# Moving a product behind the masks and scaling values earlier, at the border of two tiles of a fused attention and SwiGLU kernel

## The chip, the cores and the metric

The kernel runs on one core of a Trainium2 chip. The metric is the device time of one execution in microseconds (us). Before the change it is 238.01 us, the median of three runs (237.95 to 238.2).

## What is computed

The reference has two stages. The first is linear attention with a decay for each head, over q, k and v of shape (4, 8, 768, 64) (batch, heads, positions, head size) and a vector lam of 8 decays, in blocks of 64 positions:

```
for b in range(nb):
    intra = einsum('bhic,bhjc->bhij', qb, kb) * Dmask
    intra = einsum('bhij,bhjd->bhid', intra, vb)
    inter = einsum('bhid,bhde->bhie', qb * lam_pow, kv_state)
    out[:, :, sl] = intra + inter
    kb_dec = kb * rev_pow
    kv_state = lam_block * kv_state + einsum('bhsd,bhse->bhde', kb_dec, vb)
```

The second takes the attention's output as 3072 tokens of 512 numbers and applies a feed-forward stage of width 1536: `(silu(x @ w_gate) * (x @ w_val)) @ w_out`. The result is 3072 x 512 in float32. The kernel may choose its own block length, since a longer block gives the same sums.

## The kernel before

**Tiles.** The 768 positions are cut into six tiles of 128 positions. A tile holds all four batches, which the code calls blocks b = 0 to 3, so it has 512 tokens. Heads are kept in pairs: `kbd` and `vbd` hold k and v of a pair in a block-diagonal form, in three slots that the tiles use in turn. The first two tiles (tt = 0 and 1) are computed as one block of 128 positions, the later four as two halves of 64.

**Attention of a tile**, block by block:
- `prep_k` and `prep_q` turn k and q with TensorE (PE) in the first three tiles, or two for q; later tiles are turned by transposing transfers, issued on SP's queue by `turn` (L230, L234). `scale` multiplies the turned q by powers of the decay on VectorE (DVE), giving `qt` (L222, L224).
- `front` multiplies k and q on PE into `sp` in PSUM (L256, L258; from the third tile on L247) and masks it on DVE into `ssb` (L260; L249). The PSUM pool of `sp` has two buffers; for a block of the first two tiles `front` uses both.
- `values` adds what the state gives (`kvb`, L277; L272) and what the masked scores give (`vbd`, L278, L280; L273) into `op`, and ScalarE (ACT) copies it to `xt`, the input of the feed-forward stage (L287). For the last block of a tile of the first two, the copy is split: ACT copies two of four head pairs (L284) and DVE the other two (L285). DVE's half waits for ACT's.
- The state: `scale_v` multiplies v by powers of the decay into `v_s` (L300), two instructions to a block, on DVE for the first two tiles and on GpSimd (POOL) for the later ones. `update` multiplies k and `v_s` on PE into `up` (L313), DVE adds it to the decayed state `kvd` (L317) and decays it again (L321), and `cast_kv` copies it to `kvb` on ACT (L325). From the third tile on, `update_mid` (L333, L336) and `update_end` (midd L353, kv L355, kvd L357) do this for the two halves.

**Feed-forward of a tile.** `ffn_fc` is called twelve times, for 128 of the 1536 columns each: four gate matmuls into `gp` (L369), SiLU on ACT into `sil` (L371), four value matmuls into `vp` (L374), and the product of the two on DVE into `h_sb` (L375). `gp` and `vp` take turns in a PSUM pool of three buffers. `ffn_out` is called for each block: twelve matmuls into `ffn_op` (L384), a copy on ACT into `osb` (L387) and a transfer out on SP's queue (L388).

**The order is written out by hand.** The pools of tiles are managed, and waits are derived from them, but each engine runs its instructions in the order in which the program issues them. For each tile the loop makes a list of units: the twelve `ffn_fc`, and from the second tile on, after every third, one `ffn_out` of the tile before. So the second tile's units are 0, 1, 2: `ffn_fc`; 3: `ffn_out`; 4, 5, 6: `ffn_fc`; 7: `ffn_out`, and so on to 15. Behind each unit it issues the pieces of attention that a table names for that unit. The table `first` holds those of the first tile's units, `second` those of the second's. Pieces in them work ahead: at the end of `first` stand `front` and `values` of the second tile (L449), and from unit 4 of `second` on, the third tile's attention begins (`turn`, then `spread`).

In `second`, before the change, each block's `scale_v` is issued one or two units ahead of its `update`:

```
for b, (s0, s1) in enumerate(((0, 1), (1, 3), (3, 4), (4, 5))):
    add(second, s0, scale_v, 1, b)
    add(second, s1, update, 1, b)
    add(second, s1 + 1, cast_kv, b)
```

In the first tile's last unit, `ffn_fc` issues its `h_sb` product at once, in front of `front` for blocks 2 and 3 of the second tile, which are pieces of that unit (`first[11]`).

POOL's queue issues all loads, each waiting for the transfer eight before it, and the products of `scale_v` from the third tile on. Its order is: v of the second tile, `w_out`, k, q and v of the third tile, `scale_v` of the third tile's blocks 0 and 1, k and q of the fourth tile, `scale_v` of the third tile's blocks 2 and 3, v of the fourth, and so on.

Of the kernel before, what the change touches and what calls it, by code (L numbers as in the profile page):

```python
# [21 lines left out]
def kernel(  # L22
# [24 lines left out]
    FC = DFF // 128  # L47
# [48 lines left out]
    def load_tile(tt, order, b0=0, b1=B):  # L96
        for t in order:
            if t is q:
                if b0 == 0:
                    qn[tt] = load.tile([128, B, H, D], BF16, name="q_nat", tag="q_nat")  # L100
                load_q(tt, b0, b1)
            else:
                for c in range(2):
                    load_bd(t, kbd if t is k else vbd, tt, c, b0, b1)
# [93 lines left out]
    def xt_of(tt):  # L198
        if tt not in xts:
            xts[tt] = xpool.tile([128, MC, TT], BF16, name="xt", tag="xt")  # L200
        return xts[tt]
# [89 lines left out]
    def scale_v(tt, b):  # L291

        v_s = att.tile([128, HP, 2, D], BF16, name="v_s", tag="v_h" if tt >= HALF else "v_s")
        for h, ps in enumerate(HALVES):
            vb = vbd[ps, tt % SLOTS, 0, b * HP, 64 * h:64 * h + 64]
            eng = nc.gpsimd if tt >= HALF else nc.vector
            n = 1 if tt == NBLK - 1 else 2
            pv = bap(pw[ps], [[7, HP], [0, n], [0, D]], extra_offset=3) if tt >= HALF else \
                bap(pw[ps], [[7, HP], [1, n], [0, D]], extra_offset=2)
            eng.tensor_tensor(out=v_s[ps, :, 0:n], in0=bap(vb, [[128, HP], [128 * NP, n], [1, D]]), in1=pv,  # L300
                              op=ALU.mult)
        scaled[tt, b] = v_s
# [54 lines left out]
        nc.vector.tensor_tensor(out=kvd[b], in0=kvn[b], in1=lam64, op=ALU.mult)  # L357


    hs = {}  # L360

    def ffn_fc(tt, fc):
        xt = xt_of(tt)
        if fc == 0:
            hs[tt] = hpool.tile([128, FC, TT], BF16, name="h_sb", tag="h")
        fs = slice(fc * 128, (fc + 1) * 128)
        gp = gpsum.tile([128, TT], FP32, name="gp", tag="g")
        for mc in range(MC):
            nc.tensor.matmul(gp, wg_sb[:, mc, fs], xt[:, mc, :], start=(mc == 0), stop=(mc == MC - 1))  # L369
        sil = opool.tile([128, TT], BF16, name="sil", tag="sil")  # L370
        nc.scalar.activation(sil, gp, AF.Silu)  # L371
        vp = gpsum.tile([128, TT], FP32, name="vp", tag="g")
        for mc in range(MC):
            nc.tensor.matmul(vp, wv_sb[:, mc, fs], xt[:, mc, :], start=(mc == 0), stop=(mc == MC - 1))  # L374
        nc.vector.tensor_tensor(out=hs[tt][:, fc, :], in0=sil, in1=vp, op=ALU.mult)  # L375

    def ffn_out(tt, b, i=0, parts=1):

        w = DM // parts
        cs = slice(i * w, (i + 1) * w)  # L380
        t0 = b * S + tt * BLK
        op = apsum.tile([128, w], FP32, name="ffn_op", tag="a")
        for fc in range(FC):
            nc.tensor.matmul(op, hs[tt][:, fc, b * BLK:(b + 1) * BLK], wo_sb[:, fc, cs],  # L384
                             start=(fc == 0), stop=(fc == FC - 1))
        osb = opool.tile([128, w], FP32, name="osb", tag="osb")
        nc.scalar.copy(out=osb, in_=op)  # L387
        nc.sync.dma_start(out=out[t0:t0 + BLK, cs], in_=osb)  # L388
# [32 lines left out]
    def add(at, i, *piece):  # L421
        at.setdefault(i, []).append(piece)

    def spread(tt, at, slots):

        for b, (s0, s1, s2, s3, s4) in enumerate(slots):
            if tt >= TURNED:
                add(at, s0, scale_q, tt, b)
            else:
                add(at, s0, prep_k, tt, b)  # L430
                add(at, s1, scale_q, tt, b)
            add(at, s1, update_mid, tt, b)
            add(at, s2, cast_mid, b)
            add(at, s2, front, tt, b)
            add(at, s2, update_end, tt, b)
            add(at, s3, values, tt, b)
            if tt + 1 < NBLK:
                add(at, s4, cast_kv, b)

    first = {}  # L440
# [5 lines left out]
    for i, f, b in ((7, prep_k, 0), (8, prep_k, 1), (8, prep_q, 0), (9, prep_k, 2), (9, prep_q, 1), (9, front, 0),  # L446
                    (10, front, 1), (10, prep_q, 2), (10, prep_k, 3), (10, prep_q, 3)):
        add(first, i, f, 1, b)
    first[11] = [(front, 1, 2), (values, 1, 0), (front, 1, 3), (values, 1, 1), (values, 1, 2), (values, 1, 3, True)]  # L449
    second = {}  # L450
    for b, (s0, s1) in enumerate(((0, 1), (1, 3), (3, 4), (4, 5))):
        add(second, s0, scale_v, 1, b)
        add(second, s1, update, 1, b)
        add(second, s1 + 1, cast_kv, b)

# [2 lines left out]

    for tt in range(NBLK):
        units = [(ffn_fc, tt, fc) for fc in range(FC)]  # L460
        if tt:
            units = sum([units[3 * b:3 * b + 3] + [(ffn_out, tt - 1, b)] for b in range(B)], [])
        pieces = {}
        if tt < 2:
            pieces = (first, second)[tt]
        elif tt + 1 < NBLK:
            spread(tt + 1, pieces, [(i - 1, i, i + 1, i + 2, i + 3)
                                    for i in ((2, 5, 9, 12) if tt == 2 else (1, 4, 8, 12))])
        if 0 < tt < NBLK - 1:
            for b in range(2):  # L470
                scale_v(tt + 1, b)
            if tt + 2 < NBLK:
                load_tile(tt + 2, (k, q) if tt == 1 else (v, k, q))
            for b in range(2, B):
                scale_v(tt + 1, b)
            if tt == 1:
                load_tile(3, (v,))
        if tt and TURNED <= tt + 2 < NBLK:
            for part, i in enumerate((9, 10, 12) if tt == 1 else (5, 6, 8)):
                add(pieces, i, turn, tt + 2, part)  # L480
        for i, (f, *at) in enumerate(units):
            f(*at)
            for g, *on in pieces.get(i, []):
                g(*on)
# [34 lines left out]
```

## Time and profile before

| what | value |
|---|---|
| median of three runs | 238.01 us (237.95 to 238.2) |
| the profiled execution: its own time | 238.19 us |
| its span, from the first to the last instruction | 236.4 us |
| granted TensorE clock | 1.0 of full speed |
| PE, busy share of the span | 93% |
| DVE, ACT, POOL, busy share | 52%, 52%, 44% |
| chain that ended last, share of PE | 72% |

The profile is of one execution. Its page gives the busy time of each engine and the chain of work that ended last. Questions to its trace give instructions in order of time (start in us, duration in us, engine, line of the code, operation, output and inputs, and in brackets the idle time before it and what ended it), and waits in total (who waited for whom, us, times, longest). PE's times are modelled: a matmul's shown end lies later than the moment at which the next can start, so that matmuls overlap in the list. Rows of the same kind that follow each other are merged into one, with x and their number.

### The profile page before, as it was taken

How to read it: one execution, taken by the hardware profiler on the slowest of the kernel's cores; microseconds unless marked ns; L12 is line 12 of the kernel's file. 1: busy time of each engine (PE TensorE's matmuls, PEld its weight loads, DVE VectorE, ACT ScalarE, POOL GpSimd, SP SyncE). 2: the span in 40 equal slices, each digit the busy share in tenths (PEclk: the TensorE clock that was granted, in tenths of full speed). 3: DMA queues.
4: the chain of work that ended last, by engine and by line, in shares of the span. 5: the costliest groups of instructions: out<-in, count | busy, mean ns of one | idle time of the engine just before them, and what ended most of it. 6: DMA issues, size and time to landing. Idle time of an engine off the chain costs nothing.

```text
span 236.4 us, 4384 instructions
## 1 busy us (share of the span) xinstructions
PE 220.3 (93%) x1708; PEld 116.3 (49%) x1708; DVE 122.1 (52%) x234; ACT 123.1 (52%) x233; POOL 104.1 (44%) x129
## 2 busy tenths in 40 slices
PE   0498999989899999999999999999999999999994
PEld 0384446734455554554554555554555544444443
DVE  6685796757827954566466447336334412322200
ACT  7775669535576964645644644553634532243112
POOL 7999979962399539999942202200000000000000
PEclk9999999999999999999999999999999999999999
DMA  6999999999959998999999655110110110111032
GB/s 105 192 158 193 206 162 144 142 185 155 188 74 142 175 204 114 169 159 193 146 171 112 133 110 115 47 40 5 47 44 0 47 44 0 44 47 44 16 120 90
DMA packets 105189, 26.51 MB, mean 112 GB/s; under 512 B 96336, under 2 KB 102224, under 8 KB 105168
## 3 DMA queue, kind: packets, MB, share of 16 engines
q0 software_dynamic: 76464, 13.64, 76.1%
q1 hardware_dynamic: 28560, 12.59, 23.4%
q8 instruction: 13, 0.21, 0.4%
q14 instruction: 8, 0.07, 0.1%
q10 hardware_dynamic: 144, 0.00, 0.0%
HBM read 28.32 MB, written 6.29 MB: 146 GB/s over the span
## 4 chain that ended last, share of the span: by engine, by line
PE 72%; DMA 13%; POOL 7%; DVE 3%; issue 1%; ACT 1%; POOLq 0%; ACTq 0%; DVEq 0%
PE ffn_op L384 26%; PE vp L374 20%; PE gp L369 20%; DMA wv_sb<-in_moe_w_val_dram 6%; DMA wo_sb<-in_moe_w_out_dram 5%; DMA vbd<-in_v_dram 2%; POOL vbd L86 2%; POOL kbd L86 2%; DVE v_s L300 2%; PE sp L247 1%; PE op L272 1%; PE op L273 1%; POOL wg_sb L192 1%; PE up L333 1%; POOL wv_sb L192 1%
## 5 line engine op out<-in xcount | busy, mean ns | idle before, releaser
L375 DVE TENSOR_TENSOR h_sb<-sil,vp 128x512 bf16<-128x512 bf16 x72 | 49.3, 687 | 86.0 <-PE vp L374 60.5
L369 PE MATMUL gp<-xt,wg_sb 128*128 128x512 bf16 x288 | 74.0, 379 | 1.0 <-ACT xt L284 0.9
L374 PE MATMUL vp<-xt,wv_sb 128*128 128x512 bf16 x288 | 73.9, 379 | 0.0
L371 ACT ACTIVATE sil<-gp 128x512 bf16<-128x512 f32 x72 | 43.0, 597 | 44.2 <-PE gp L369 42.5
L384 PE MATMUL ffn_op<-wo_sb,h_sb 128*128 128x512 bf16 (+1 forms) x300 | 65.5, 371 | 0.0
L300 POOL TENSOR_TENSOR v_s<-vbd,pw 64x512 bf16<-64x512 bf16 (+1 forms) x32 | 30.4, 950 | 42.2 <-PE up L333 26.0
L374 PEld LDWEIGHTS <-wv_sb 128*128 128x128 bf16 x288 | 28.2, 98 | 34.0
L384 PEld LDWEIGHTS <-h_sb 128*128 128x128 bf16 x300 | 28.3, 98 | 29.5
L387 ACT COPY osb<-ffn_op 128x512 f32<-128x512 f32 (+1 forms) x25 | 14.2, 568 | 52.1 <-PE ffn_op L384 52.1
L369 PEld LDWEIGHTS <-wg_sb 128*128 128x128 bf16 x288 | 25.5, 98 | 25.2 <-issue 1.1
L86 POOL DMA_DIRECT2D vbd<-in_v_dram x32 | 24.2, 795 | 2.0 <-DMA wo_sb<-in_moe_w_out_dram 1.8
L86 POOL DMA_DIRECT2D kbd<-in_k_dram x28 | 22.1, 821 | 2.5 <-DMA wv_sb<-in_moe_w_val_dram 1.7
L287 ACT CAST xt<-op 128x512 bf16<-128x512 f32 x22 | 12.9, 586 | 8.8 <-PE op L273 5.1
L325 ACT CAST kvb<-kv 64x256 bf16<-64x256 f32 x40 | 16.1, 403 | 0.8
L209 ACT CAST ktb<-tk 64x512 bf16<-64x512 f32 x24 | 13.9, 579 | 2.5 <-PE tk L207 2.2
L341 ACT CAST kvb<-mid 64x256 bf16<-64x256 f32 x32 | 12.9, 403 | 0.5
L249 DVE TENSOR_TENSOR ssb<-sp,mask 128x512 bf16<-128x512 f32 x16 | 11.0, 684 | 2.8 <-PE sp L247 2.8
L300 DVE TENSOR_TENSOR v_s<-vbd,pw 64x512 bf16<-64x512 bf16 x16 | 10.9, 683 | 0.2
L214 PE MATMUL tq<-identity,q_nat 128*128 128x128 bf16 x32 | 4.0, 262 | 6.8 <-POOL identity masks.py:199 6.3
L272 PE MATMUL op<-qt,kvb 128*128 128x64 bf16 x128 | 9.8, 193 | 0.1
L273 PE MATMUL op<-ssb,vbd 128*128 128x64 bf16 x128 | 9.8, 193 | 0.0
L272 PEld LDWEIGHTS <-kvb 128*128 128x128 bf16 x128 | 8.7, 98 | 2.1 <-ACT kvb L341 0.2
(78 smaller groups left out, 185.8 us busy)
## 6 DMA issues: line engine op xcount, KB each, us to landing
out_dram<-osb SPq DMA_DIRECT2D x23, 256.0 KB, 2.1
kbd<-in_k_dram POOLq DMA_DIRECT2D x20, 128.0 KB, 6.0
q_nat<-in_q_dram POOLq DMA_DIRECT2D x4, 512.0 KB, 11.0
vbd<-in_v_dram POOLq DMA_DIRECT2D x16, 128.0 KB, 8.2
wo_sb<-in_moe_w_out_dram POOLq DMA_DIRECT2D x1, 1536.0 KB, 13.1
q_raw<-in_q_dram SPq DMA_DIRECT2D x4, 256.0 KB, 5.4
vbd<-in_v_dram POOLq DMA_DIRECT2D x16, 64.0 KB, 4.5
wg_sb<-in_moe_w_gate_dram POOLq DMA_DIRECT2D x2, 512.0 KB, 10.5
```

Source lines behind the costliest of these rows:

```text
L86: nc.gpsimd.dma_start(out=dst[ps, tt % SLOTS, c, b0 * HP:b1 * HP, 64 * h:64 * h + 64], in_=bass.AP(tensor=t.tensor, offset=t.offset + ((b0 ...
L209: nc.scalar.copy(out=ktb[ps, tt % 2, :, b * HP:(b + 1) * HP, 64 * h:64 * h + 64], in_=tk[ps])
L272: nc.tensor.matmul(op[:, hp, cs], kvb[:, c, b, hp, :], qt[:, hp, cs], start=True, stop=False)
L287: nc.scalar.copy(out=xt, in_=op)
L300: eng.tensor_tensor(out=v_s[ps, :, 0:n], in0=bap(vb, [[128, HP], [128 * NP, n], [1, D]]), in1=pv, op=ALU.mult)
L325: nc.scalar.copy(out=kvb[ps, 0, b, :, 64 * h:64 * h + 64], in_=kvn[b][ps])
L369: nc.tensor.matmul(gp, wg_sb[:, mc, fs], xt[:, mc, :], start=(mc == 0), stop=(mc == MC - 1))
L371: nc.scalar.activation(sil, gp, AF.Silu)
L374: nc.tensor.matmul(vp, wv_sb[:, mc, fs], xt[:, mc, :], start=(mc == 0), stop=(mc == MC - 1))
L375: nc.vector.tensor_tensor(out=hs[tt][:, fc, :], in0=sil, in1=vp, op=ALU.mult)
L384: nc.tensor.matmul(op, hs[tt][:, fc, b * BLK:(b + 1) * BLK], wo_sb[:, fc, cs], start=(fc == 0), stop=(fc == FC - 1))
L387: nc.scalar.copy(out=osb, in_=op)
```

## The change

`ffn_fc` is split into `ffn_gv` (gate, SiLU, value) and `ffn_h` (the product into `h_sb`); calling it does both, as before. For the first tile's last unit only `ffn_gv` is called, and its `ffn_h` is issued in `first[11]`, behind `front` of blocks 2 and 3 and `values` of blocks 0 to 2, in front of `values` of block 3. `scale_v` of the second tile's blocks 0 and 1 is issued at the end of `first[11]`, that is ahead of the second tile's units; that of block 2 behind unit 0 and that of block 3 behind unit 2. The updates move one unit forward: from behind units 1, 3, 4, 5 to behind units 0, 2, 3, 4, and their casts with them.

On PE, the four groups of `up` matmuls stand one unit earlier than before and all else keeps its order. On DVE, `h_sb` of the first tile's last unit stands behind four masks; four scalings stand in front of the second tile's first `h_sb`, and the other four behind the first and the second update's instructions. On ACT, the casts stand a unit earlier. The orders on POOL and SP are the same as before. No instruction is added or left out.

```diff
-    hs = {}
-
-    def ffn_fc(tt, fc):
+    hs, gv = {}, {}
+
+    def ffn_gv(tt, fc):
         xt = xt_of(tt)
         if fc == 0:
             hs[tt] = hpool.tile([128, FC, TT], BF16, name="h_sb", tag="h")
...
             nc.tensor.matmul(vp, wv_sb[:, mc, fs], xt[:, mc, :], start=(mc == 0), stop=(mc == MC - 1))
+        gv[tt, fc] = sil, vp
+
+    def ffn_h(tt, fc):
+        sil, vp = gv.pop((tt, fc))
         nc.vector.tensor_tensor(out=hs[tt][:, fc, :], in0=sil, in1=vp, op=ALU.mult)
+
+    def ffn_fc(tt, fc):
+        ffn_gv(tt, fc)
+        ffn_h(tt, fc)
...
-    first[11] = [(front, 1, 2), (values, 1, 0), (front, 1, 3), (values, 1, 1), (values, 1, 2), (values, 1, 3, True)]
+    first[11] = [(front, 1, 2), (values, 1, 0), (front, 1, 3), (values, 1, 1), (values, 1, 2), (ffn_h, 0, FC - 1),
+                 (values, 1, 3, True), (scale_v, 1, 0), (scale_v, 1, 1)]
     second = {}
-    for b, (s0, s1) in enumerate(((0, 1), (1, 3), (3, 4), (4, 5))):
-        add(second, s0, scale_v, 1, b)
+    for b, (s0, s1) in enumerate(((None, 0), (None, 2), (0, 3), (2, 4))):
+        if s0 is not None:
+            add(second, s0, scale_v, 1, b)
         add(second, s1, update, 1, b)
         add(second, s1 + 1, cast_kv, b)
...
         units = [(ffn_fc, tt, fc) for fc in range(FC)]
-        if tt:
+        if tt == 0:
+            units[-1] = (ffn_gv, 0, FC - 1)
+        else:
             units = sum([units[3 * b:3 * b + 3] + [(ffn_out, tt - 1, b)] for b in range(B)], [])
```

## The prediction, as put on record before the run

> **What bounds the kernel now.** I read the page's busy times first, then the waits of PE in the stretch that the change touches, then the order of time of PE, DVE and POOL there.
>
> ```profile
> PE 220.3 (93%) x1708; PEld 116.3 (49%) x1708; DVE 122.1 (52%) x234; ACT 123.1 (52%) x233; POOL 104.1 (44%) x129
> ...
> PE up L313 <- DVE v_s L300: 1.7, 3, 0.7
> PE gp L369 <- ACT xt L284: 0.5, 1, 0.5
> PE sp L256 <- DVE ssb L260: 0.4, 1, 0.4
> PE sp L247 <- DVE qt L224: 0.3, 1, 0.3
> ```
>
> TensorE is busy for 93% of the span, so only a shorter PE wait saves time. The four lower lines are all that PE's matmuls wait for between 43 and 83 us (who is waited for, us in total, times, longest). Before 43 and after 83 us the change leaves every engine's order as it is. The first and third of them are what the change touches.
>
> In order of time, PE's five waits at the border of the first two tiles (start, duration, what ran, idle time in brackets):
>
> ```profile
> 45.15 0.22 PE L256 MATMUL sp<-qt,ktb 128*128 128x128 bf16 x1 [0.41 <-DVE ssb L260]
> 48.09 1.05 PE L369 MATMUL gp<-xt,wg_sb 128*128 128x512 bf16 x4 [0.46 <-ACT xt L284]
> 52.17 0.41 PE L313 MATMUL up<-v_s,kbd 128*128 128x64 bf16 x8 [0.44 <-DVE v_s L300]
> 59.42 0.41 PE L313 MATMUL up<-v_s,kbd 128*128 128x64 bf16 x8 [0.56 <-DVE v_s L300]
> 62.23 0.39 PE L313 MATMUL up<-v_s,kbd 128*128 128x64 bf16 x8 [0.68 <-DVE v_s L300]
> ```
>
> The brackets count from the modelled end of a matmul. Undisturbed, a gate or value pass of four matmuls gives way to the next 0.86 us after its start (the steps of the chain of waits), though its last matmul ends at 1.03. So a wait costs about 0.17 more than its bracket: the three of `up` cost 0.61 (52.17 less 50.70 and 0.86), 0.73 and 0.85 us.
>
> DVE over the same time:
>
> ```profile
> 43.94 0.69 DVE L375 TENSOR_TENSOR h_sb<-sil,vp 128x512 bf16<-128x512 bf16 x1 [0.46 <-PE vp L374]
> 44.54 2.00 DVE L260 TENSOR_TENSOR ssb<-sp,mask 128x384 bf16<-128x384 f32 x4
> 48.07 0.42 DVE L285 CAST xt<-op 128x256 bf16<-128x256 f32 x1 [1.53 <-ACT xt L284]
> 50.11 0.69 DVE L375 TENSOR_TENSOR h_sb<-sil,vp 128x512 bf16<-128x512 bf16 x1 [1.61 <-PE vp L374]
> 50.72 1.40 DVE L300 TENSOR_TENSOR v_s<-vbd,pw 64x512 bf16<-64x512 bf16 x2
> 60.78 1.40 DVE L300 TENSOR_TENSOR v_s<-vbd,pw 64x512 bf16<-64x512 bf16 x2
> ```
>
> Each scaling pair ends 0.05 to 0.06 us before the `up` that waited for it. DVE does not lack time: it idles 1.53 and 1.61 us just before the first pair.
>
> **The change, step by step.** No instruction is added or removed; the orders of SP's and POOL's queues are the same. What changes is places.
>
> (1) The first tile's last h_sb goes behind the masks of blocks 2 and 3. Block 2's first mask then starts when its scores end, 43.81 + 0.19 + 0.04 = 44.04, instead of 44.54. The scores of block 3 wait for that mask to free their PSUM buffer, so they come at 44.65 (PE's preceding values end at 44.57). The values, ACT's copies of xt and the first gate pass follow in the same lockstep: 48.09 becomes 47.59. Saved: 0.50. The h_sb itself now runs at about 46.1 to 46.8, in the 1.53 us in which DVE waits for ACT; its readers (the first output matmuls) come after 53 us, and the PSUM buffer it holds is next wanted at 49.6. Without that idle time it would cost its 0.61 on the xt copy.
>
> (2) Four scaling instructions (blocks 0 and 1) now follow that xt copy at once. DVE: copy 47.57, scalings 47.91 to 50.75 (two pairs by 1.42). The v they read had landed: PE itself read all blocks of it from 44.01 to 47.44. The first `up` follows the gate and value passes at 49.34 instead of waiting to 52.17: its pair is done at 49.31, release 0.05, so 0.02 of 0.61 is left. Saved: 0.59.
>
> (3) Blocks 2 and 3 are scaled well ahead. By adding the rows in the new order, block 2's pair is done at 53.6 and its `up` is due behind the first output matmuls at 56.05; block 3's is done at 57.0, its `up` due at 58.0. Saved: 0.73 + 0.85.
>
> (4) A new wait: the first h_sb of the second tile stands behind the four scalings, so it starts at 50.75 instead of 49.65, and ends 51.44. The third gate pass takes the PSUM buffer that it frees; PE is there at 51.33 and goes on at 51.49. Cost: 0.16. Its bounds: 0 (there is no such wait now) to 1.08, if the scalings ran at 0.91 us each, the longest row of another 512-element bf16 product, qt; all 16 rows of L300 on DVE lie between 676 and 690 ns, so I take 0.16.
>
> Sum at the sixth gate pass: 0.50 + 0.59 + 0.73 + 0.85 - 0.16 = 2.51 us; 62.46 becomes 59.95.
>
> (5) What is late next. Things set by transfers don't move. The third tile's k has landed by 57.5 (issued 47, 9.5 to landing) and is wanted at 61.7; its turned q lands at 67.3 and is wanted at 67.6; v_s of its block 2 leaves POOL at 74.5 and PE wants it at 74.4, which costs 0.1 inside a wait of 0.26 for kvb that is there anyway. The fourth tile's turned q lands at 90.0 when DVE comes for it, some 3 us before PE needs it. These cost nothing.
>
> (6) But DVE now meets POOL elsewhere:
>
> ```profile
> 72.21 4.61 POOL L300 TENSOR_TENSOR v_s<-vbd,pw 64x512 bf16<-64x512 bf16 x4
> ...
> 72.67 0.86 DVE L353 TENSOR_TENSOR midd<-mid,pw 128x256 f32<-128x256 f32 x1
> 74.03 0.70 DVE L357 TENSOR_TENSOR kvd<-kv,pw 128x256 f32<-128x256 f32 x1
> 75.25 0.67 DVE L224 TENSOR_TENSOR qt<-qt,qsc 128x512 bf16<-128x512 bf16 x1
> 77.69 0.41 DVE L353 TENSOR_TENSOR midd<-mid,pw 128x256 f32<-128x256 f32 x1
> 78.60 0.43 DVE L357 TENSOR_TENSOR kvd<-kv,pw 128x256 f32<-128x256 f32 x1
> ```
>
> The same instruction takes 0.41 us alone and 0.86 while POOL multiplies. In POOL's three long stretches of products (72.2 to 76.8, 99.4 to 108.3, 116.6 to 121.1) all eight DVE instructions with both inputs in SBUF are longer, by 0.25 to 0.77 us; those that read PSUM are not. POOL's stretch is set by transfers and stays. The midd, kvd and qt of block 1/2 that ran clear at 77.69 to 79.36 come 2.5 us sooner, at 75.2 to 76.9: midd and at least part of kvd inside it. I take 0.3 to 0.45 for midd and 0 to 0.28 for kvd, together 0.3 to 0.73. The chain has 0.15 us of slack (an h_sb waiting for ACT at 79.76), and then ends in the one place where PE already waits for DVE:
>
> ```profile
> 82.21 0.42 DVE L224 TENSOR_TENSOR qt<-qt,qsc 128x512 bf16<-128x512 bf16 x1
> 82.68 0.39 PE L247 MATMUL sp<-qt,ktb 128*128 128x64 bf16 x8 [0.28 <-DVE qt L224]
> ```
>
> So 0.15 to 0.58 of the gain is given back there; I take 0.46, nearer the upper end because midd's three contended rows (0.86, 0.73, 1.18) are all long. The instructions that leave POOL's stretch (72.67, 74.03) gain PE nothing: it is in output matmuls then.
>
> The Trainium skill, "SBUF — State Buffer", section "Who interferes with whom", has a rule that speaks against the change here: a DVE instruction with two SBUF inputs contends with a GpSimd instruction that reads SBUF, and the loser is blocked for the other's whole instruction. The eight rows agree on who contends, but lengthen by less than a whole POOL product (1.04 to 1.13 us). By that rule my estimate is that midd and kvd would lose about 1.2 us together and the time would be some 236.5; by the rows it is 236.0.
>
> **Sum.** 2.51 - 0.46 = 2.05 us off. The profiled execution took 238.19 us (span 236.4 and 1.8 around it), so 236.14; it lies 0.18 above the median of the runs, 238.01, from which 2.05 leaves 235.96. Predicted: 236.0 us.
>
> **Rivals.**
> Full gain: POOL and DVE don't meet, or the lost time is hidden. For it: kvd and qt are at the edge of POOL's stretch. Against it: eight of eight rows. 238.01 - 2.51 = 235.5.
> Head of the queue: the four scalings hold back the first h_sb for longer, as POOL issues transfers at 48 to 51.4 us. At 0.91 each, 0.92 more: a gain of 1.1, 236.9. Against it: the pair at 50.72 ran beside such issues at its usual 0.68.
> It does nothing: PE's gaps close but the third tile's transfers or POOL's v_s catch PE and take it all back: 238.0. Against it: the dates in (5); only the 0.1 us is missed.
> Slower: the same h_sb behind the four scalings. The savings without it are 2.67 us, so it decides once PE waits longer for that buffer, that is from 0.71 + 0.63 = 1.34 us per scaling on. No row of L300 is so long, POOL's own included (1.135 at most). At 1.5 each, 238.6.
>
> **Chances.** Forecast 0.60 (own range 235.7 to 236.3); full gain 0.17; head of the queue 0.13; nothing 0.05; slower 0.05. A measurement of this kernel can tell 0.2%, 0.48 us, from no change; the head case lies mostly beyond that (0.11 of 0.13). So faster 0.88, same 0.07, slower 0.05. The range, 235.4 to 236.9, reaches from the full gain to the price of the head case.
>
> **What would show it.** (1): the first gate pass of the second tile near 47.6. (2), (3): no PE wait for v_s at L313 above 0.1. (4): a wait of about 0.16 of L369 for h_sb. (6): midd near 75.2 at 0.7 us or more, and PE's wait for qt at L247 grown from 0.28. What would make it wrong: scalings on DVE longer than 0.69, or a PE wait for a transfer or for POOL in the third tile.

## The result, and the profile after

The changed kernel takes 236.47 us, the median of 22 runs (235.49 to 242.68), against 238.14 us for the kernel before on the same chip (22 runs, 237.7 to 239.71). The ratio is 0.9928 [0.9909, 0.9947]: some 1.7 us off, where 2.05 was predicted. The ratio leaves out the three longest runs of the changed kernel (239.22 to 242.68 us), of which the longest had a lower granted clock (0.993). Two more series of the changed kernel, below, gave 0.9929 and 0.9924. The time lies inside the predicted range. What is to be explained is a gain about a third of a microsecond short (the 2.05 itself lies inside each interval), and runs that spread more than before: the median lies 0.98 us above the lowest run after the change and 0.44 before it, and from lowest to lowest the gain is 2.21 us (237.70 to 235.49).

The profiled execution of the changed kernel took 235.49 us (span 233.7). That is the shortest of its 22 runs, 2.70 us less than the profiled execution before. So this profile shows the change at its best, not at its median. The page's busy times, and all of PE's waits between 43 and 83 us:

```profile
PE 217.8 (93%) x1679; PEld 115.7 (50%) x1708; DVE 121.3 (52%) x234; ACT 123.2 (53%) x233; POOL 104.4 (45%) x129
```

```profile
PE gp L369 <- ACT xt L284: 0.5, 1, 0.5
PE sp L247 <- DVE qt L224: 0.3, 1, 0.3
```

Of the four lines of before, the two that the change touches are gone: `up` for v_s (1.7 us in three waits) and `sp` for ssb (0.4). The count of PE's matmuls is smaller only because 29 records are missing from the trace; the 1708 weight loads are all there. In order of time on PE (start, duration, what ran, idle time before it):

```profile
47.25 1.05 PE L369 MATMUL gp<-xt,wg_sb 128*128 128x512 bf16 x3 [0.46 <-ACT xt L284]
...
49.02 0.41 PE L313 MATMUL up<-v_s,kbd 128*128 128x64 bf16 x8
...
50.13 1.03 PE L374 MATMUL vp<-xt,wv_sb 128*128 128x512 bf16 x4
51.16 1.02 PE L369 MATMUL gp<-xt,wg_sb 128*128 128x512 bf16 x4
...
59.62 1.03 PE L369 MATMUL gp<-xt,wg_sb 128*128 128x512 bf16 x4
...
79.99 0.39 PE L247 MATMUL sp<-qt,ktb 128*128 128x64 bf16 x8 [0.29 <-DVE qt L224]
```

The first line is the first gate pass of the second tile (48.09 before). The first `up` follows at once. The step from 50.13 to 51.16 is 1.03 us where an undisturbed one is 0.86: 0.17 us of a new wait, too short for the view to put in brackets. 59.62 is the sixth gate pass (62.46 before), 79.99 the place where PE waits for qt (82.68 before). DVE beside it:

```profile
45.62 0.68 DVE L379 TENSOR_TENSOR h_sb<-sil,vp 128x512 bf16<-128x512 bf16 x1
...
47.57 2.81 DVE L300 TENSOR_TENSOR v_s<-vbd,pw 64x512 bf16<-64x512 bf16 x4
50.41 0.69 DVE L379 TENSOR_TENSOR h_sb<-sil,vp 128x512 bf16<-128x512 bf16 x1
...
74.85 0.45 DVE L353 TENSOR_TENSOR midd<-mid,pw 128x256 f32<-128x256 f32 x1
...
75.79 0.70 DVE L357 TENSOR_TENSOR kvd<-kv,pw 128x256 f32<-128x256 f32 x1
```

The held-back h_sb runs at 45.62, in idle time. The four scalings take 2.81 us together, their usual length, and the second tile's first h_sb follows them at 50.41. The last two lines are the midd and kvd that were to meet POOL's products: 0.45 and 0.70 us, against 0.41 and 0.43 in the clear before.

The difference of 2.70 us between the two profiled executions closes. 0.35 us had been won before the change begins (the scores of block 2 start at 43.32 against 43.67). From there to the first gate pass 0.49 is saved (3.93 against 4.42), from that to the sixth gate pass 2.00 (12.37 against 14.37), and up to the qt wait 0.15 is given back (20.37 against 20.22). That makes 2.34 us for the change and 2.69 with the head start.

### The profile page after: what moved, and what is told of

It is laid out like the page before. It is cut to its first block, busy times and chain, and to the rows that moved or that the text cites. A ratio compares the mean times of both kernels' runs of the same rounds, so it can differ in the third digit from the quotient of the medians.

```text
span 233.7 us, 4354 instructions
## 1 busy us (share of the span) xinstructions
PE 217.8 (93%) x1679; PEld 115.7 (50%) x1708; DVE 121.3 (52%) x234; ACT 123.2 (53%) x233; POOL 104.4 (45%) x129
## 4 chain that ended last, share of the span: by engine, by line
PE 85%; DVE 6%; DMA 2%; ACT 2%; issue 2%; POOL 1%; ACTq 0%; DVEq 0%; POOLq 0%
PE ffn_op L392 26%; PE gp L369 24%; PE vp L374 24%; DMA kbd<-in_k_dram 2%; PE sp L247 2%; PE op L273 1%; PE op L272 1%; PE up L333 1%; DVE h_sb L379 1%; PE tk L207 1%; PE sp L256 1%; POOL kbd L86 1%; DVE v_s L300 1%; DVE ssb L260 1%; ACT xt L287 1%
## 5 line engine op out<-in xcount | busy, mean ns | idle before, releaser
L369 PE MATMUL gp<-xt,wg_sb 128*128 128x512 bf16 x277 | 72.8, 379 | 1.7 <-ACT xt L284 0.9
L374 PE MATMUL vp<-xt,wv_sb 128*128 128x512 bf16 x282 | 72.9, 379 | 0.1
L392 PE MATMUL ffn_op<-wo_sb,h_sb 128*128 128x512 bf16 (+1 forms) x288 | 64.2, 370 | 0.6
## 6 DMA issues: line engine op xcount, KB each, us to landing
wo_sb<-in_moe_w_out_dram POOLq DMA_DIRECT2D x1, 1536.0 KB, 12.7
```

## The experiments

Each ratio is against runs of the kernel before on the same chip. The theory at the start: the change's steps are as predicted, and the runs that are longer than the profiled one lose time to transfers, for which PE now comes too early. Its rivals were that one half of the change does all the work, that the new wait for h_sb costs more than it seems, and that DVE's meeting with POOL takes the rest. First the two halves, a second look and the new wait.

**Masks alone.**

```diff
-                 (values, 1, 3, True), (scale_v, 1, 0), (scale_v, 1, 1)]
+                 (values, 1, 3, True)]
-    for b, (s0, s1) in enumerate(((None, 0), (None, 2), (0, 3), (2, 4))):
+    for b, (s0, s1) in enumerate(((0, 1), (1, 3), (3, 4), (4, 5))):
```

> The first tile's last h_sb stands behind the masks as in the changed kernel; the scalings and updates of the second tile stand where they were before the change. Theory (the savings are waits of TensorE, one by one): the first gate pass of the second tile comes 0.5 us sooner, the three waits of up for v_s stay at 0.6, 0.7 and 0.85 us, and the time falls by 0.5 us, to about 237.6. Rival (the masks' earlier start is taken back by ACT's copies of xt): the gate pass comes no sooner and the time stays at 238.1.

Measured: 237.85 us, ratio 0.9996 [0.9977, 1.0015]. In its profile the wait for ssb is gone, and block 2's scores lead to the first gate pass in 3.92 us instead of 4.42, the same 0.5 as in the whole change. The three waits of `up` stay as before (0.44, 0.56, 0.68). So the step is shown in the trace; in the time, half a microsecond is 0.2% and the interval is as wide, so it can't be told from no change.

**Scalings alone.**

```diff
-    first[11] = [(front, 1, 2), (values, 1, 0), (front, 1, 3), (values, 1, 1), (values, 1, 2), (ffn_h, 0, FC - 1),
+    first[11] = [(ffn_h, 0, FC - 1), (front, 1, 2), (values, 1, 0), (front, 1, 3), (values, 1, 1), (values, 1, 2),
```

> The scalings and updates stand as in the changed kernel; the first tile's last h_sb stands in front of the masks as before the change. Theory: the first gate pass comes when it came before, the waits of up for v_s go, a wait of 0.17 us of the third gate pass for h_sb comes, about 0.15 us is given back in the third tile, so 1.85 us off: 236.3. Rival (the two parts need each other, since the scalings start earlier only if the xt copy does): under 1 us off, over 237.1.

Measured: 237.02 us, 0.9945 [0.9914, 0.9977]. The wait for ssb is back (0.41) and no `up` of the second tile waits for DVE. So this half brings most of the gain, though 0.7 us less than expected. Its profiled execution, 239.42 us, has two waits that no profile before had: `up` of the third tile's block 2 stands 0.98 us for v_s from POOL, and `up` of the fourth tile's block 0 stands 2.17 us for the same.

**The changed kernel, profiled again.**

> The changed kernel, unaltered, for a second profile and more times. The first profiled execution was 2.7 us shorter than that of before, the median of the runs only 1.7. Theory (the rest of the gain hangs on transfers, which differ from execution to execution): an execution near the median, 236.4, shows PE, DVE or POOL waiting for a transfer in the second or third tile where the first profile had none, 0.5 to 1 us of it. Rival (the whole program runs a little slower in some executions): no new wait, the difference spread over the span.

Measured: 236.94 us, 0.9929 [0.9904, 0.9954]; the profiled execution took 238.42 us, its span 2.9 us more than that of the first one. The same program, so the two profiles can be laid side by side. PE's waits that the first doesn't have, in order of time:

```profile
54.07 2.55 PE L392 MATMUL ffn_op<-wo_sb,h_sb 128*128 128x512 bf16 x11 [0.82 <-DMA wo_sb<-in_moe_w_out_dram]
...
75.61 0.39 PE L333 MATMUL up<-v_s,kbd 128*128 128x64 bf16 x8 [0.44 <-ACT osb L395]
...
78.54 0.39 PE L247 MATMUL sp<-qt,ktb 128*128 128x64 bf16 x8 [0.33 <-DVE qt L224]
...
93.11 0.39 PE L333 MATMUL up<-v_s,kbd 128*128 128x64 bf16 x8 [1.10 <-POOL v_s L300]
```

The first gate pass starts at 47.23 here and at 47.25 there. The sixth is 0.97 us later (60.59), after the wait for w_out. At the third tile's block 2 PE is 1.57 later (75.61 against 74.04). The wait for qt at 78.54 stands behind a midd and a kvd that POOL lengthened; by PE's next wait for qt it has cost 0.09 (81.65 against 79.99, 1.66 later). The fourth tile's first `up` is 2.93 later (93.11 against 90.18); its v loads stand behind the second four on POOL's queue, and go out 1.66 later (77.81 against 76.15). That is the whole difference of the spans. The second line names ACT, but that osb copy had long been done; the wait ends with POOL's products, as POOL's order of time shows, first of the changed kernel's first profile, then of this one:

```profile
52.58 1.77 POOL L86 DMA_DIRECT2D vbd<-in_v_dram  x2 [1.38 <-DMA wo_sb<-in_moe_w_out_dram]
62.28 4.38 POOL L300 TENSOR_TENSOR v_s<-vbd,pw 64x512 bf16<-64x512 bf16 x4 [7.94 <-DMA vbd<-in_v_dram]
...
71.67 4.54 POOL L300 TENSOR_TENSOR v_s<-vbd,pw 64x512 bf16<-64x512 bf16 x4
```

```profile
54.31 1.75 POOL L86 DMA_DIRECT2D vbd<-in_v_dram  x2 [2.69 <-DMA wo_sb<-in_moe_w_out_dram]
64.04 4.38 POOL L300 TENSOR_TENSOR v_s<-vbd,pw 64x512 bf16<-64x512 bf16 x4 [7.98 <-ACT ktb L209]
...
73.42 4.44 POOL L300 TENSOR_TENSOR v_s<-vbd,pw 64x512 bf16<-64x512 bf16 x4
```

Here the cause can be read. POOL's next v load waits for w_out to land (a load waits for the transfer eight before it). w_out took 12.7 us from issue to landing in the one execution, 14.0 in the other, and was issued 0.48 later. So the v loads go out 1.73 us later, the first products start 1.76 later, and the second four 1.75 later; where PE waits, its `up` starts 2.19 us behind these. Across executions, in us (the last column is the idle time of that `up`; a dash, where it did not wait):

| profiled execution | v load freed by w_out | first product | second four | `up` of block 2 | idle |
|---|---|---|---|---|---|
| before | 53.16 | 62.40 | 72.21 | 76.88 | - |
| masks alone | 54.81 | 64.65 | 74.03 | 77.32 | - |
| changed, first | 52.58 | 62.28 | 71.67 | 74.04 | - |
| changed, second | 54.31 | 64.04 | 73.42 | 75.61 | 0.44 |
| scalings alone | 53.97 | 63.86 | 73.64 | 75.83 | 0.98 |

With 2.19 us behind the start of the second four, the slack at this `up` was 2.5 us before (76.88 - 72.21 - 2.19) and 1.1 with the masks alone, in an execution whose second four came 1.8 us later. In the changed kernel it is 0.2 at best. So at this `up` the order of before hides a late w_out, and the changed one shows it.

**Two scalings ahead of the units instead of four.**

```diff
-                 (values, 1, 3, True), (scale_v, 1, 0), (scale_v, 1, 1)]
+                 (values, 1, 3, True), (scale_v, 1, 0)]
-    for b, (s0, s1) in enumerate(((None, 0), (None, 2), (0, 3), (2, 4))):
+    for b, (s0, s1) in enumerate(((None, 0), (0, 2), (1, 3), (2, 4))):
```

> The changed kernel, but only block 0 is scaled ahead of the second tile's units; block 1's two scalings stand behind the first update's instructions, block 2's and 3's one unit later. Theory (h_sb behind four scalings costs the third gate pass 0.17 us): that wait goes, no wait of up comes in its place, and fc5's gate pass stands 0.17 us sooner than in the changed kernel; the time falls by 0.15, to about 236.2. Rival (the order of DVE is now too tight and up waits for block 1's or 3's scaling): a wait of up for v_s of 0.2 us or more.

Measured: 236.66 us, 0.994 [0.9906, 0.9974]. The third gate pass starts at 50.99 instead of 51.16, from the same 47.25, so the wait of 0.17 us is gone and no `up` of the second tile waits. The time shows nothing of it: the waits for w_out (0.20) and POOL (0.54 and 1.87) are there. The new wait for h_sb is as small as it was taken to be, and it is not what is missing.

Next, the cause itself: take traffic away, give POOL's products more time, and take the meeting of DVE and POOL away.

**The changed kernel with half of w_out.** Half of it is loaded and used twice.

```diff
-            nc.tensor.matmul(op, hs[tt][:, fc, b * BLK:(b + 1) * BLK], wo_sb[:, fc, cs],
+            nc.tensor.matmul(op, hs[tt][:, fc, b * BLK:(b + 1) * BLK], wo_sb[:, fc % (FC // 2), cs],
-    nc.gpsimd.dma_start(out=wo_sb, in_=moe_w_out.rearrange("(c p) m -> p c m", p=128))
+    nc.gpsimd.dma_start(out=wo_sb[:, 0:FC // 2], in_=moe_w_out.rearrange("(c p) m -> p c m", p=128)[:, 0:FC // 2])
```

> The changed kernel, with only the first half of w_out loaded and used in place of the second half too: 0.75 MB less to move before the third tile's k, q and v, on transfer engines that are busy without a break from 40 to 60 us. Theory (in most executions the change's gain is cut by transfers that land too late, since TensorE now comes 2.5 us sooner): the loads land some 4 us sooner, no PE wait for w_out, up or v_s of the third and fourth tile is left, the times draw together near the best of the changed kernel, median 235.4 to 235.8. Rival (the long executions are a slower program as a whole): median as the changed kernel's, 236.5 to 236.9, with as wide a spread.

Measured: 235.62 us (six runs, 235.38 to 236.0), 0.989 [0.9868, 0.9912]. w_out lands in 8.8 us, POOL's products start at 59.34 and 68.79, and PE waits only for xt (0.46) and qt (0.28), as in the best execution of the changed kernel. The median goes down to what had been the fastest runs, and the spread from several microseconds to 0.6. So it is the late transfers that the longer runs of the changed kernel wait for.

**The kernel before with half of w_out.** The same two lines, in the kernel before.

> The kernel before with the same half of w_out loaded and used twice, as the other side of the comparison. Theory (before the change, TensorE comes late enough for nearly all transfers): the time stays within 0.4 us of before, 237.8 to 238.2, so that the change is worth 2.3 us or more without the transfers. Rival (the kernel before is held by transfers just as well): it falls by as much as the changed kernel does, 0.8 us or more.

Measured: 242.43 us (240.93 to 243.94), 1.0171 [1.0132, 1.021]. It was to gain or stay; it loses 4 us with less to transfer. In order of time, on POOL, DVE and PE:

```profile
58.29 4.91 POOL L300 TENSOR_TENSOR v_s<-vbd,pw 64x512 bf16<-64x512 bf16 x4 [5.28 <-DMA vbd<-in_v_dram]
...
57.85 2.13 DVE L300 TENSOR_TENSOR v_s<-vbd,pw 64x512 bf16<-64x512 bf16 x2
...
62.21 2.25 DVE L300 TENSOR_TENSOR v_s<-vbd,pw 64x512 bf16<-64x512 bf16 x2
...
60.04 0.41 PE L313 MATMUL up<-v_s,kbd 128*128 128x64 bf16 x8 [1.30 <-DVE v_s L300]
64.52 0.39 PE L313 MATMUL up<-v_s,kbd 128*128 128x64 bf16 x8 [2.34 <-DVE v_s L300]
...
83.50 0.39 PE L247 MATMUL sp<-qt,ktb 128*128 128x64 bf16 x8 [1.47 <-DVE qt L224]
```

Since v of the third tile lands sooner, POOL's products (58.3 to 63.2) fall upon DVE's last scalings of the second tile. A pair takes 2.13 to 2.25 us instead of 1.40, and the two waits of `up` grow from 0.56 and 0.68 to 1.30 and 2.34. Later products lengthen a qt (1.26 us), and PE waits 1.47 for it at block 2 of the third tile, where it did not wait before; the wait at block 3 stays (0.29 for 0.28). These three make nearly all of the 3.9 us by which the span is longer (0.74 + 1.66 + 1.47). In the changed kernel the same scalings end at 56.6, before POOL begins even with the half load (59.3). The comparison of the two half loads therefore needed another run, below.

**The third tile's `up` a unit later.**

```diff
-                                    for i in ((2, 5, 9, 12) if tt == 2 else (1, 4, 8, 12))])
+                                    for i in ((3, 6, 9, 12) if tt == 2 else (1, 4, 8, 12))])
```

> The changed kernel, with the fourth tile's pieces of blocks 0 and 1 issued one unit later among the third tile's units (from behind units 2 and 5 to behind 3 and 6). Theory (in the longer executions up of the fourth tile's block 0 waits 1.1 to 2.2 us for v_s, that is for v's transfer): that wait goes whatever the execution, the one for the third tile's block 2 (0.4 to 1.0 us) stays; median 0.4 to 1 us below the changed kernel's, about 236.0. Rival (the wait only moves to the next piece that needs the transfers): no change.

Measured: 236.38 us, 0.9936 [0.991, 0.9962]. The wait at the fourth tile doesn't show in this execution, though w_out landed in 13.3 us; the one at block 2 of the third does (0.46). The time can't be told from the changed kernel's: the 0.4 to 1 us that were expected don't show. It settles nothing.

**POOL's second four products of the third tile as memsets.** The values of its blocks 2 and 3 are not scaled but set to zero, in a like time on POOL.

```diff
+            if tt == 2 and b >= 2:
+                for _ in range(2):
+                    nc.gpsimd.memset(v_s[ps], 0.0)
+                continue
```

> The changed kernel, with POOL's products for the third tile's blocks 2 and 3 replaced by two memsets each of about the same length, which write but don't read; these two blocks' v_s are left out. Theory (DVE instructions with two inputs in SBUF are lengthened by POOL's reads): midd, kvd and qt of the third tile take 0.41 to 0.42 us each instead of 0.45, 0.70 and 1.10 in the first profile of the changed kernel, and between fc5's gate pass and block 3's scores PE loses nothing more than before the change; 0.15 us at most of the time. Rival (any work of POOL lengthens them, by its writes): they stay as long as they were.

Measured: 236.72 us, 0.9927 [0.9902, 0.9951]. In order of time, on POOL and DVE:

```profile
73.30 4.51 POOL L302 MEMSET v_s<- 64x512 bf16 x8
...
75.57 0.41 DVE L357 TENSOR_TENSOR midd<-mid,pw 128x256 f32<-128x256 f32 x1
...
76.47 0.42 DVE L361 TENSOR_TENSOR kvd<-kv,pw 128x256 f32<-128x256 f32 x1
```

POOL is busy over the same stretch, but reads no SBUF, and midd and kvd have their clear lengths; in the second profile of the changed kernel they took 1.14 and 0.70 there. (In this kernel the lines stand four further down.) PE does not wait for qt at all. So it is POOL's products that lengthen DVE's, not POOL's being busy (the section on the prediction shows by how much). The time is no better, because this profile still waits for w_out (0.38) and for POOL (0.66 and 0.58).

Last, a remedy for the waits on POOL, a third look at the changed kernel, and the pair for the half load.

**POOL scales block 2 before it issues k and q of the fourth tile, and `up` comes later.**

```diff
-                                    for i in ((2, 5, 9, 12) if tt == 2 else (1, 4, 8, 12))])
+                                    for i in ((4, 7, 9, 12) if tt == 2 else (1, 4, 8, 12))])
-            for b in range(2):
+            ahead = 3 if tt == 1 else 2
+            for b in range(ahead):
...
-            for b in range(2, B):
+            for b in range(ahead, B):
```

> The changed kernel with room for late transfers: POOL scales the third tile's block 2 ahead of issuing the fourth tile's k and q (2.2 us sooner for v_s, 2.2 us later for these loads), and the fourth tile's pieces of blocks 0 and 1 stand two units later (from behind units 2 and 5 to behind 4 and 7). Theory (the waits of up for POOL's v_s in the third and fourth tile are what takes the gain back): neither wait is left in any execution, median 235.6 to 236.0, and few times over 236.5. Rival (the loads that now come later, q of the fourth tile above all, are waited for instead): a PE wait for qt or ktb of the fourth tile, median 236.4 or more.

Measured: 237.47 us, 0.9948 [0.9918, 0.9978]. PE waits for no v_s any more, as meant. But the last two products, which now start at 74.79, lie beside the qt of block 2, which takes 1.26 us instead of 0.42, and PE waits 0.79 for it, where the first profile has no wait. Two smaller waits for qt stand later, where no other profile so far has one: 0.18 at 108.80, behind another lengthened qt, and 0.28 at 126.65, behind a transfer of q. The remedy failed: it trades one wait for others.

**The changed kernel, a third time.**

> The changed kernel, unaltered, beside the two variants on the same chip, and for a third profile. Both theories: median 236.4 to 237.0; PE waits for v_s of POOL or for w_out only in an execution in which these land later than in the first profile.

Measured: 237.07 us, 0.9924 [0.9897, 0.9951]; its profiled execution, 236.45 us, is of the three the nearest to the median of the 22 runs. w_out took 13.7 us, the v load went out at 53.44, the products started at 63.34 and 72.72, and `up` of block 2 waited 0.60 (74.91, again 2.19 behind). From the first gate pass of the second tile to the first tile's last output pass (block 3's) this execution is 1.04 us longer than the first profiled one (36.20 against 35.16), and its span is 0.9 longer.

**The kernel before with half of w_out, and POOL's products of the third and fourth tile as memsets.** The half load as above, and:

```diff
+            if tt in (2, 3):
+                for _ in range(2):
+                    nc.gpsimd.memset(v_s[ps], 0.0)
+                continue
```

> The kernel before with half of w_out, which was 4 us slower than before, with POOL's products of the third and fourth tile replaced by memsets of the same length, so that these tiles' v_s are left out. Theory (with less to move, POOL's products fell on the second tile's scalings on DVE and lengthened them from 0.7 to as much as 1.5 us): the scalings are back at 0.68, the waits of up for v_s at 0.4 to 0.7, and the time at 237.4 to 238.1. Rival (the sooner transfers themselves, or their clash with the transposes, made it slow): the time stays over 240.

Measured: 237.85 us (237.77 to 238.12), 0.9976 [0.9961, 0.9991]. All 16 scalings on DVE take 0.676 to 0.690 us again, the waits of `up` are 0.44, 0.56 and 0.69, and the loss of 4 us is gone. So it was DVE's meeting with POOL's products. The memsets read no v and so wait for no transfer: they run at 53.4 to 57.9, beside three of the second tile's scalings, and the fourth tile's v goes out 4.9 us sooner than with the half load alone (67.63 against 72.51), which costs nothing either. With w_out's lateness out of the way on both sides, the change is worth 237.85 - 235.62 = 2.2 us. That comparison is rough: the two were run on different chips, whose kernels before differ by 0.2, and only the side of before has the memsets.

**The remedy with two scalings ahead of the units.** The edits of the two kernels above together.

> The variant with room for late transfers, and in it only block 0 scaled ahead of the second tile's units, so that the third gate pass doesn't wait for h_sb. Theory: the sum of both, 0.15 us below the variant without: 235.5 to 235.9. Rival (DVE's order is too tight with two scalings later): a PE wait for v_s on DVE, no gain over it.

Measured: 237.29 us, 0.9953 [0.9927, 0.998]. No gain over the remedy alone. Its profiled execution (241.77 us) was the longest of its twelve runs, so no times are read from it. None of the variants that compute all of the work is faster than the changed kernel.

## Why the prediction was right, and where it failed

- **(1) Masks.** Right: 0.50 predicted, 0.49 measured, and 0.50 with this half alone.
- **(2), (3), (4) Scalings and the new wait.** Right together: 0.59 + 0.73 + 0.85 - 0.16 = 2.01 predicted from the first to the sixth gate pass, 2.00 measured. The new wait was 0.17 for 0.16, and went when two scalings were moved instead of four.
- **(6) DVE meets POOL.** The mechanism was right, the size was not: 0.46 was taken, and 0.15 was given back, the lower bound (0.09 more in the second profile). The signs named for it, a midd of 0.7 us or more and a longer wait for qt, are not in the first profile (0.45 and 0.29). The rows have a rule that I missed. POOL's product that runs beside midd and kvd in the first profile of the changed kernel, then midd and the product beside it in the second:

```profile
75.08 1.13 POOL L300 TENSOR_TENSOR v_s<-vbd,pw 64x512 bf16<-64x512 bf16 x1
```

```profile
75.82 1.14 DVE L353 TENSOR_TENSOR midd<-mid,pw 128x256 f32<-128x256 f32 x1
...
75.64 1.04 POOL L300 TENSOR_TENSOR v_s<-vbd,pw 64x512 bf16<-64x512 bf16 x1
```

  The product of the first fence ends at 76.21. kvd (75.79) starts 0.42 us before that end and is lengthened by 0.28. The product of the second ends at 76.68; midd (75.82) starts 0.86 before that end and is lengthened by 0.73. The midd of the first profile (74.85) starts 0.17 before the end of the product in front, 75.02, and is lengthened by 0.04. Each time the lengthening is what is left of the running product less some 0.13 us. In the profile of before and ten profiles after it (all but those with memsets and the last), all 85 DVE products with both inputs in SBUF that start more than 0.14 us before the end of a running POOL product follow this, with 0.123 to 0.140 us for the 0.13 (against clear lengths of 0.41 for midd, 0.42 for kvd and qt, 0.68 for `v_s`). What these 0.13 us are isn't shown. The ten that start before the product that they meet are not lengthened (0.006 at most); there the product is, to 1.31 us at most. By the rows of before the term could have been worked out, but only from the moment at which each instruction starts: 0.04 + 0.28, less the 0.15 of slack, is 0.17. A shift of POOL by half a microsecond gives another number: in the third profile midd starts 0.03 after the start of a product and takes 1.30.
- **(5) "Things set by transfers don't move ... These cost nothing".** This is the step that failed. I read when each transfer landed from one execution and set those dates against a PE that was 2.5 us sooner. But a date is spread over 1 to 2 us from one execution to the next, and the change had used up the slack that hid this: at the third tile's block 2, I had found POOL done at 74.5 and PE there at 74.4, and put it down as hidden. Waits for w_out (0.2 to 0.8 us in brackets), for v_s of the third tile (0.4 to 1.0) and of the fourth (0.6 to 2.2) are what the longer of the profiled executions have more, up to 2.9 us in one. A wait of PE for POOL in the third tile was one of the signs named for a wrong prediction; the first profile has none, the second and third have one. Without this step the forecast would have come out too careful: 2.34 us in the best execution, some 2.2 with w_out's lateness out of the way, for 2.05. So it is in part luck that the time came out within half a microsecond: (6) took some 0.3 us too much from the gain, and (5) some 0.6 us too little.
- **The rivals.** "Head of the queue" and "slower" fell: the four scalings took 2.81 us, their usual time, with no product of POOL near. "Full gain" came near in the fastest runs alone. "It does nothing: ... transfers or POOL's v_s catch PE" named the right mechanism, but as all or nothing; it takes a part in most executions and nearly all in some.
- **The rule weighed against the rows.** The Trainium skill, "SBUF — State Buffer", section "Who interferes with whom", calls the shared ports an exclusive lock: the one that issues first holds them for its whole instruction, and the other is fully blocked. The prediction put this aside, because the rows lengthen by less than a whole product. That was a misreading: the block lasts to the end of the product that is running, and a DVE instruction usually meets it on its way. The 85 rows, the ten that came first, and POOL's memsets, beside which nothing is lengthened, agree with the page, but for the 0.13 us, of which it says nothing. That the 236.5 estimated by the misread rule is what was measured (236.47) is chance: the meeting gave back 0.15 us, not 1.05 (1.2 less the slack of 0.15).

What stays open is why w_out takes 12.7 us in one execution and 14.0 in another of the same program; the half load shows only that less traffic takes the effect away. At the fourth tile, 1.5 us of the delay of POOL's first product (89.23 against 87.72) is handed on from the third; the next product is 3.0 us later (92.01 against 88.97), and the second half of that was not tried by itself.

## What to carry to other kernels

A date that a transfer sets is a range over executions, not a number: before PE is brought forward, write down the slack at each place that waits for a transfer or for an engine fed by one, and treat what falls below the spread of the dates (here 1 to 2 us) as a cost, not as hidden. One profile can be the fastest of 22 runs, so look at a second before explaining a median. And where DVE and POOL both read SBUF, price a meeting by what is left of the instruction that came first; a transfer that lands sooner can then cost more than it saves, by setting the one's products beside the other's.

## What had not been expected of the hardware

Halving one load made the kernel before 4 us slower, through nothing but the time at which POOL's products started. And the price of a meeting of DVE and POOL was sharper than thought: to within 0.01 us the rest of the running product less 0.13, so that the same midd took between 0.41 and 1.30 us for a shift of at most a microsecond.
